# Strided attention and a two-layer MLP on one core: six attention outputs to a bank, first v casts on GpSimd, and the seven-product form one block earlier

## The chip, the core and the metric

The kernel runs on one core of a Trainium2 chip. The core has five engines that work side by side, each with its own queue of instructions taken in order: TensorE (PE in the profile; its weight loads are PEld), VectorE (DVE), ScalarE (ACT), GpSimd (POOL) and SyncE (SP). POOL and SP issue DMAs; POOL's DMAs here load and convert float32 to float16, SP's store the output and transpose tiles on the way. Engines wait for each other through semaphores. The metric is the device time of one execution in microseconds (us).

## What is computed

Eight batches of eight heads, 576 positions of 64 values. Heads 0 to 3 attend to the last 32 positions ("local"), heads 4 to 7 to every earlier position with the same remainder mod 32 ("strided"). The result, with the heads laid side by side, is the input of an MLP:

```
scores = scale * np.matmul(q, k.transpose(0, 1, 3, 2))
...
scores = np.where(masks[None, :, :, :], scores, -1000000000.0)
scores = scores - np.max(scores, axis=-1, keepdims=True)
attn = np.exp(scores)
attn = attn / (np.sum(attn, axis=-1, keepdims=True) + 1e-09)
return np.matmul(attn, v).astype(np.float32)
...
h = x @ w_in
r = np.maximum(h, 0.0)
g = s * (r * r) + b
return (g @ w_out).astype(np.float32)
```

Here x is 4608 x 512, w_in 512 x 2048, w_out 2048 x 512.

## The kernel before

**Attention.** A batch b is worked in four pairs of heads, m = 0 and 1 local, m = 2 and 3 strided; the pair is called (b, m). q and k are brought into transposed form, on PE (`trans`, L427) for the first batches and by DMA transposes from SP for the later ones: `k_dma` (L487, tiles kT_loc, kT_alt, kTs, kT), `q_dma` (L509, tiles qTl, qT). `score` (L551) multiplies them, ACT takes the exponential, and `av` (L614) multiplies by v. v has a column of ones, so the product also holds the sum of the row. A strided pair has 2 heads x 8 tiles of 72 positions. In `av` four tiles of one head go to one PSUM bank (`per = nt // 2`), so a pair is four groups; for each group DVE takes a reciprocal (`rc`) and multiplies (`mu`) into x_nat. A local pair has two groups of six tiles of 96 positions.

**x for the MLP.** x_nat has to be transposed into xT. For local pairs from batch 2 on a DMA does it (`x_dma`, L699). For strided pairs of batches 4 to 6 x_nat is written to DRAM (`x_out`, L691, tile x_dram) and read back transposed (`x_in`, L695); all others, batch 7's strided pairs among them, are transposed on PE (`xtrans`, L665) with one PSUM bank and a copy.

**MLP.** Tokens come in nine blocks T of 512. `ff1` (L904) is 64 matmuls of 512 columns a block; ACT applies the relu, ACT or DVE the square, giving gT. The second product has two forms. `ff2` (L962) is 64 matmuls of 512 columns, with one eviction for each of four row tiles. `ff2_seven` (L784), used from block SEVEN = 3 on, is a Strassen-like form: gT and w_out are cut in quarters, and seven products P1 to P7 of 16 matmuls of 256 columns replace eight. It needs sums of quarters of gT (`sums_post`, L738, eight DVE adds a block, tile S and places in gT), mixed weights (`mix_post`, L768, four DVE subtractions made once; w_mix1 overwrites a quarter of w_out), and eight DVE evictions and adds a block.

**Loads.** POOL's queue is written in order: q, k and v of batch 0, the casts of v_loc (`cast_v`, L362), w_in, then (function `second`) q, k, v of batch 1 and w_out. Later, per batch: a one-element copy `gate` (L1042) that waits until the previous batch's strided k has been transposed by DMA, then ql, kl, qs, ks (`load_qk`), v_loc and v_str. v of the strided heads of batches 0 to 3 lands in a tile vs and is copied to v_str (`cast_v`); for batch 0 ACT or DVE makes that copy.

**Order.** What stands after what on each engine is decided while the kernel is built: `Plan` keeps a clock for PE and a time at which each engine is free, takes steps when their inputs should be ready, and gives a piece of work to the engine that would end it first. It holds estimated costs (`posts`) and arrival times (`AT`, `landing`). Attention steps are paced against MLP steps by `due` (L1223). Where nothing is ready in the first 16 MLP steps, `keep_running` (L1199) puts in dummy matmuls on constants. A change of an estimate can thus reorder all five queues, and SP's queue is in order: a store or a transpose that is not ready holds up all behind it.

Of the kernel before, what the change touches and what calls it, by code (L numbers as in the profile page):

```python
# [10 lines left out]
FP32 = mybir.dt.float32  # L11
# [4 lines left out]
class Plan:  # L16
# [107 lines left out]
def kernel(  # L124
# [237 lines left out]
    def cast_v(b, loc, mm, key):  # L362
        nt, np_, dst = (LT, 128, v_loc) if loc else (ST, SQ, v_str)

        def g(eng):
            src = vl_stage if loc else loaded[b, "vs"].rearrange(
                "p (h t d) -> p h t d", h=4, d=D)
            for h in range(2 * mm, 2 * mm + 2):
                copy_on(eng, out=dst[b % NV][0:np_, h, :, 0:D], in_=src[:, h])
        n = nt * D  # L370
        plan.post([key], {"P": 1000.0} if loc else {"A": 2 * (170 + 0.83 * n), "V": 540.0,
                                                           **({"P": 1500.0} if b == 0 else {})}, g,
                  [("cast", b, mm) if loc else ("in", "vs", b, mm)])
        if loc:
            rows_before(b, mm, ("cast", b, mm))
# [37 lines left out]
    def bank(group):  # L413
        return ps[group.name]

    def pair_steps(b, m):
# [10 lines left out]
        def trans(name, j, group):  # L427
            alone = loc and b < HEAD_T

            def f():  # L430
                if j == 0:
                    st["p" + name] = bank(group).bitcast(FP16)[:, 0:S]
                if alone:
                    for e in range(2):
# [12 lines left out]
            s = Step(f, 70 if alone else 35, needs=[("in", name + sfx, b, mm)],  # L447
                     group=group if j == 0 else None)
            if j == nt - 1:
                key = ("t", name, id_)  # L450
                s.keys = [key]
                if name == "q":
# [3 lines left out]
                    def g(eng):  # L456
                        ps, qD = st["pq"], st["q"]
                        for e in range(2):
# [5 lines left out]
                            else:  # L464
                                copy_on(eng, out=qD[hs, :, e, :],
                                        in_=ps[hs].rearrange("d (j p) -> d j p", j=nt))
                    s.posts = [([key], {"A": 1280, "V": 1520 if loc else 918}, g,
                                [("q", id_), group])]
                else:
                    def g(eng):  # L470
# [5 lines left out]
                        else:  # L476
                            st["k"] = qkp.tile([128, ST, SR], FP16, tag="kTs", name="kTs")
                            copy_on(eng, out=st["k"][:, :, 0:SQ],
                                    in_=st["pk"].rearrange("d (j p) -> d j p", j=nt))
                    s.posts = [([key], {"A": 640, "V": 757 if loc else 453}, g, [("k", id_), group])]  # L480
            return s

        k_by_dma = b >= (KB_DMA if loc else 3)
        q_by_dma = b >= (QB_DMA if loc else QS_DMA)
        x_by_dma = b >= 2 if loc else XS_DMA <= b < B - 1

        def k_dma(eng):  # L487
            if loc:
# [62 lines left out]
        def score(i, group):  # L551
# [18 lines left out]
            if i % per_s == n - 1:  # L570
# [21 lines left out]
                free = [("a", (b - 1, m), 1, nt - 1)] if b else []  # L592
# [18 lines left out]
        per = nt if loc else nt // 2  # L611
        vt = (v_loc if loc else v_str)[b % NV]

        def av(e, j, group):  # L614
            def f():
                if j == 0 and e == 0:
                    st["x"] = xnp.tile([nq, nt, 128], FP16, tag="x" + sfx, name="x_nat")
                if j % per == 0:
                    st["a"] = bank(group)[:, 0:6 * (D + 1)].rearrange("p (j d) -> p j d", d=D + 1)
                g, i = p_of(e, j)  # L620
                nc.tensor.matmul(  # L621
                    out=st["a"][:, j % per, :], lhsT=st["pw", g][0:nk, i * nq:i * nq + WIDE],
                    rhs=vt[0:nk, 2 * mm + e, j, :])
                st["pa", e, j] = st["a"]

            s = Step(f, 35, needs=[("p", id_, p_of(e, j)[0]), ("in", "v" + sfx, b, mm)],
                     group=group if j % per == 0 else None)
            if j % per == per - 1:
                key = ("a", id_, e, j)
                s.keys = [key]  # L630
                j0 = j - per + 1

                def rc(eng):
                    st["rec", e, j] = recp.tile([128, 6, 1], FP32, tag="rec", bufs=8,
                                                name="rec")
                    nc.vector.reciprocal(out=st["rec", e, j][0:nq, 0:per],  # L636
                                         in_=st["pa", e, j][0:nq, 0:per, D:D + 1])

                def mu(eng):
                    if eng == "A":  # L640
                        for i in range(per):
                            nc.scalar.activation(
                                out=st["x"][:, j0 + i, 64 * e:64 * e + 64],
                                in_=st["pa", e, j][0:nq, i, 0:D], func=AF.Copy,
                                scale=st["rec", e, j][0:nq, i])
                        return
                    nc.vector.tensor_tensor(  # L647
                        out=st["x"][:, j0:j0 + per, 64 * e:64 * e + 64],
                        in0=st["pa", e, j][0:nq, 0:per, 0:D],
                        in1=st["rec", e, j][0:nq, 0:per].to_broadcast([nq, per, D]), op=ALU.mult)  # L650

                s.posts = [([key], {"V": 185}, rc, [("r", id_, e, j)]),
                           ([("r", id_, e, j)], {"V": 150 + 1.05 * 64 * per,
                                                 **({"A": 225.0 * per} if b == 0 else {})}, mu,
                            [("x", id_, e, j), group])]
            return s

        for e in range(2):
            for j in range(nt):
                if j % per == 0:  # L660
                    gr = group_of("a", b, m)
                steps.append(av(e, j, gr))
        st["last_av"] = steps[-1]

        def xtrans(j, group):  # L665
            def f():
                if j == 0:
# [5 lines left out]
            jx = j // per * per + per - 1  # L673
            s = Step(f, 35, needs=[("x", id_, 0, jx), ("x", id_, 1, jx)],
                     group=group if j == 0 else None)
            if j == nt - 1:
                key = ("xt", id_)
# [24 lines left out]
                in_=st["x"].rearrange("p t d -> p (t d)"))  # L702

        if x_by_dma and loc:
            plan.post([("x", id_, e, nt - 1) for e in range(2)] + x_free(b), {"D": 1000.0}, x_dma,
                      [("xT", b, m)], 4000.0 if b == B - 1 else 6000.0 if b < 4 else None)
        elif x_by_dma:

            plan.post([("x", id_, e, j) for e in range(2) for j in (per - 1, nt - 1)],
                      {"X": 500.0}, x_out, [("xd", id_)])  # L710
            plan.post([("xd", id_)] + x_free(b), {"Y": 1300.0}, x_in, [("xT", b, m)])
        else:
            gr = group_of("t", b, m)
            for j in range(nt):
# [4 lines left out]
    gts = {}  # L719

    SQ_ACT = 0
    SEVEN = 3
    H = NFT // 2

    def ff_order(T):
# [42 lines left out]
    def mix_post():  # L768

        wl, wr = [[w_out_sb[:, H * j:H * j + H, 256 * k:256 * k + 256] for j in range(2)]  # L770
                  for k in range(2)]
        jobs = ((3, wr[1], wr[0]), (1, wr[0], wl[0]), (2, wr[1], w_mix[1]), (4, wl[1], w_mix[2]))
        before = [("F2", SEVEN - 1)]
        for i, x, y in jobs:
            plan.post(before, {"V": 1250.0},
                      lambda eng, i=i, x=x, y=y: nc.vector.tensor_tensor(
                          out=w_mix[i], in0=x, in1=y, op=ALU.subtract), [("w_mix", i)])
# [301 lines left out]
    def after_landing(i, src):  # L1079
# [7 lines left out]
    early_v(0)  # L1087
    plan.free["P"] = 7100.0
    plan.free["V"] = 6500.0
    AT = {"ql0": 5300.0, "kl0": 6800.0, "ql1": 7750.0, "kl1": 8750.0, "qs": 10150.0,  # L1090
          "ks": 12000.0, "vl0": 7100.0, "vl1": 13300.0, "vs": 14950.0}
    for key, at in AT.items():
        if key[:2] == "vl":
# [209 lines left out]
```

## Time and profile before

| What | us |
|---|---|
| median of 6 runs (lowest to highest) | 306.64 (305.94 to 307.32) |
| the profiled execution | 306.61 |
| its span, first to last instruction | 304.8 |
| last matmul ends, by the timeline | 300.95 |
| last store eviction on DVE ends | 301.47 |

The span is the profiler's; 1.8 us of the execution lie around it. TensorE's granted clock was 1.00 of full speed. Busy time by stage, us of each stretch:

| stretch | PE | DVE | ACT | POOL |
|---|---|---|---|---|
| 0 to 25 | 21.38 | 15.72 | 16.73 | 16.66 |
| 25 to 30 | 2.92 | 1.68 | 2.52 | 2.27 |
| 30 to 50 | 19.96 | 17.17 | 12.76 | 10.49 |
| 50 to 100 | 50.00 | 39.80 | 39.40 | 23.32 |
| 100 to 175 | 75.00 | 57.99 | 53.43 | 35.80 |
| 175 to 200 | 24.29 | 18.35 | 16.65 | 3.87 |
| 200 to 290 | 90.00 | 58.87 | 44.87 | 0 |

A matmul's record reaches from its issue to its modelled end, so records overlap and their mean length is more than the spacing at which they follow each other. For what a matmul costs in a dense stream, the spacing of starts is the number to read.

### The profile page before, as it was taken

Reading aid. Unit: us, or ns where it says so; the run is one execution under the profiler, and the core shown is the slowest. Engines: PE = TensorE matmul, PEld = TensorE weight load, DVE = VectorE, ACT = ScalarE, POOL = GpSimd, SP = SyncE. Lnnn points to the kernel's source line nnn. Section 1 sums busy time; section 2 is a strip of 40 time slices with the busy share of each in tenths; the row PEclk is TensorE's granted clock in tenths of the full one; section 3 lists DMA queues with packets and bytes.
Section 4 is the critical chain, followed back from the end, with each engine's and each line's share of the span. In section 5 each row is a group of like instructions: output and inputs, shape, how many; then the busy total and the mean of one; then the engine's idle time right before and its main releaser. Section 6 shows DMA issues by size and latency. Waiting matters only on the chain.

```text
span 304.8 us, 6780 instructions
## 1 busy us (share of the span) xinstructions
PE 294.5 (97%) x2673; PEld 205.0 (67%) x2673; DVE 216.1 (71%) x482; ACT 186.4 (61%) x331; POOL 92.4 (30%) x135
## 2 busy tenths in 40 slices
PE   7987999999999999999999999999999999999994
PEld 3763655666565667777567776678888676766884
DVE  5655896899777687548886986698766366747653
ACT  4876955889857785658497857685635454444300
POOL 8933463833940392039403940000000000000000
PEclk9999999999999999999999999999999999999999
DMA  8999999998999599999999999946010110300213
GB/s 138 160 207 201 170 209 185 208 150 140 144 151 141 69 126 144 147 171 138 133 197 165 116 141 140 186 103 128 2 37 34 69 37 0 105 0 2 97 62 120
DMA packets 101290, 37.15 MB, mean 122 GB/s; under 512 B 80858, under 2 KB 98778, under 8 KB 101258
## 3 DMA queue, kind: packets, MB, share of 16 engines
q0 software_dynamic: 58880, 18.23, 61.9%
q1 hardware_dynamic: 42378, 18.49, 33.0%
q8 instruction: 21, 0.34, 0.5%
q14 instruction: 11, 0.09, 0.1%
HBM read 36.86 MB, written 10.32 MB: 155 GB/s over the span
## 4 chain that ended last, share of the span: by engine, by line
PE 82%; DMA 12%; POOL 4%; issue 1%; DVE 0%; POOLq 0%
PE ps_f L914 35%; PE ps_f L882 18%; PE ps_f L971 13%; DMA ql<-in_q_dram 5%; PE ps_s L564 5%; DMA v_loc<-in_v_dram 4%; DMA kT_alt<-kl 3%; PE ps_a L621 3%; PE ps_s L882 2%; PE ps_t L882 1%; PE ps_s L971 1%; PE ps_t L444 1%; PE ps_t L621 1%; POOL w_in_sb L335 1%; PE ps_t L669 1%; POOL v_loc L345 1%
## 5 line engine op out<-in xcount | busy, mean ns | idle before, releaser
L914 PE MATMUL ps_f<-xT,w_in_sb 128*128 128x512 f16 (+4 forms) x696 | 148.4, 340 | 0.0
L940 ACT ACTIVATE u<-ps_f 128x512 f16<-128x512 f32 x138 | 81.4, 596 | 70.1 <-PE ps_f L914 67.1
L914 PEld LDWEIGHTS <-w_in_sb 128*128 128x128 f16 x704 | 71.8, 113 | 32.3 <-issue 0.2
L882 PEld LDWEIGHTS <-gT 128*128 128x128 f16 x512 | 48.9, 98 | 11.9
L971 PE MATMUL ps_f<-w_out_sb,gT 128*128 128x512 f16 x176 | 47.8, 379 | 0.0
L950 DVE TENSOR_TENSOR gT<-u 128x1024 f16<-128x1024 f16 x46 | 31.4, 682 | 18.6 <-ACT u L940 18.1
L882 PE MATMUL ps_f<-w_out_sb,gT 128*128 128x256 f16 x312 | 43.4, 272 | 0.0
L948 ACT ACTIVATE gT<-u 128x1024 f16<-128x1024 f16 x26 | 27.5, 1057 | 0.7
L647 DVE TENSOR_TENSOR x_nat<-ps_a,rec 72x256 f16<-72x256 f32 (+1 forms) x55 | 25.2, 459 | 0.9
L971 PEld LDWEIGHTS <-gT 128*128 128x128 f16 x192 | 17.2, 98 | 11.7 <-issue 0.4
L582 ACT ACTIVATE p_str<-ps_s 72x432 f16<-72x432 f32 (+1 forms) x47 | 21.5, 483 | 4.5 <-PE ps_s L564 4.4
L582 ACT ACTIVATE p_loc<-ps_s 128x384 f16<-128x384 f32 x46 | 21.1, 492 | 4.9 <-PE ps_s L564 4.6
L621 PEld LDWEIGHTS <-p_str 72*128 72x128 f16 x256 | 15.2, 98 | 7.5 <-ACT p_str L582 0.7
L754 DVE TENSOR_TENSOR gT<-gT 128x1024 f16<-128x1024 f16 x28 | 18.5, 682 | 1.4 <-ACT gT L948 1.3
L323 POOL DMA_DIRECT2D v_loc<-in_v_dram x24 | 17.7, 760 | 4.3 <-PE ps_a L621 1.8
L882 PE MATMUL ps_f<-w_mix,gT 128*128 128x256 f16 x144 | 18.8, 273 | 0.0
L882 PEld LDWEIGHTS <-S 128*128 128x128 f16 x160 | 15.5, 98 | 3.5
L636 DVE RECIPROCAL rec<-ps_a 72x4 f32<-72x4 f32 (+1 forms) x56 | 10.0, 179 | 9.7 <-PE ps_a L621 9.0
L328 POOL DMA_DIRECT2D v_str<-in_v_dram x16 | 13.0, 816 | 9.3 <-PE ps_f L914 5.4
L1042 POOL COPY gate<-kT 1x1 f16<-1x1 f16 x6 | 1.5, 253 | 44.6 <-DMA kT<-ks 44.6
L345 ACT COPY qD_loc<-ps_t 64x576 f16<-64x576 f16 x18 | 11.4, 632 | 5.6 <-PE ps_t L436 4.7
L882 PE MATMUL ps_f<-w_mix,S 128*128 128x256 f16 x96 | 14.4, 273 | 0.0
(163 smaller groups left out, 415.9 us busy)
## 6 DMA issues: line engine op xcount, KB each, us to landing
out_dram<-o SPq DMA_DIRECT2D x34, 256.0 KB, 2.5
w_in_sb<-in_moe_w_in_dram POOLq DMA_DIRECT2D x4, 512.0 KB, 11.0
w_out_sb<-in_moe_w_out_dram POOLq DMA_DIRECT2D x4, 512.0 KB, 11.5
qs<-in_q_dram POOLq DMA_DIRECT2D x6, 288.0 KB, 6.5
ks<-in_k_dram POOLq DMA_DIRECT2D x6, 288.0 KB, 8.1
v_loc<-in_v_dram POOLq DMA_DIRECT2D x24, 72.0 KB, 8.8
ql<-in_q_dram POOLq DMA_DIRECT2D x5, 288.0 KB, 8.0
kl<-in_k_dram POOLq DMA_DIRECT2D x16, 72.0 KB, 3.6
```

The source lines that it names most:

```text
L323: nc.gpsimd.dma_start(out=vl[LPAD:128, h, :, 0:D], in_=v_band(b, h))
L564: nc.tensor.matmul(out=st["s", g][0:nk, c:c + 2 * nq], lhsT=(st["k"][:, i * nq:i * nq + nk] if loc else st["k"][:, i, 0:SQ]), rhs=st["q"][ ...
L582: nc.scalar.activation(out=st["pw", g][0:nk, 0:2 * n * nq], in_=st["s", g][0:nk, 0:2 * n * nq], func=AF.Exp, scale=scale)
L621: nc.tensor.matmul(out=st["a"][:, j % per, :], lhsT=st["pw", g][0:nk, i * nq:i * nq + WIDE], rhs=vt[0:nk, 2 * mm + e, j, :])
L647: nc.vector.tensor_tensor(out=st["x"][:, j0:j0 + per, 64 * e:64 * e + 64], in0=st["pa", e, j][0:nq, 0:per, 0:D], in1=st["rec", e, j][0:nq, ...
L754: nc.vector.tensor_tensor(out=at(out), in0=at(x), in1=at(y), op=op)
L882: nc.tensor.matmul(out=gts[name, T, t][:, 0] if halves else gts[name, T][:, t], lhsT=lhs(k, t), rhs=rhs(k), start=fresh and k == 0 and (ha ...
L914: nc.tensor.matmul(out=gts["h", T, ft][:, lo:hi], lhsT=w_in_sb[ft // 4][:, ct].rearrange("p (x l) -> p l x", l=4)[:, ft % 4], rhs=xT[ct][: ...
L940: nc.scalar.activation(out=u, in_=gts["h", T, ft], func=AF.Relu)
L948: nc.scalar.activation(out=g, in_=u, func=AF.Square)
L950: nc.vector.tensor_tensor(out=g, in0=u, in1=u, op=ALU.mult)
L971: nc.tensor.matmul(out=gts[id_], lhsT=gts[T][:, ft, ts * 128:(ts + 1) * 128], rhs=w_out_sb[:, ft, cols], start=(ft == 0), stop=(ft == NFT ...
```

## The change

Six edits:

1. In `cast_v` the copies of batch 0's strided v (vs to v_str, four of 72x512) are offered to POOL alone. In the built order they stand on POOL's queue after the four w_in loads and the v_loc copy, and before the loads of batch 1.
2. The copies of q of pair (0, 1) and of k of pair (0, 0) are given to DVE alone.
3. `keep_running` puts in dummies of at least 128 columns into each gap before 9.6 us of the plan's clock. The early estimates (`AT`, the cost of a transpose) are retouched. There are 30 dummy matmuls in the built order instead of 19.
4. Strided outputs: the 16 tiles of a pair go to banks as 6, 6 and 4, in the order n, with the two heads alternating, so a pair has three groups instead of four. x_nat is written across both heads.
5. `XS_DMA <= b` without `< B - 1`: batch 7's strided pairs also go through x_dram, with two stores and two transposing loads on SP in place of 16 transposes on PE.
6. SEVEN = 2: block 2 takes the seven-product form. `mix_post` makes w_mix3, w_mix2 and w_mix4 after block 0's second product and w_mix1 after block 1's.

```diff
-                w = r + self.LATER.get(k[0] if isinstance(k, tuple) else None, 0.0)
+                w = r + self.LATER.get(k[0] if isinstance(k, tuple) and k[2:3] != (0,) else None, 0.0)
...
-        plan.post([key], {"P": 1000.0} if loc else {"A": 2 * (170 + 0.83 * n), "V": 540.0,
-                                                           **({"P": 1500.0} if b == 0 else {})}, g,
+        plan.post([key], {"P": 1000.0} if loc else {"P": 1160.0} if b == 0 else {"A": 2 * (170 + 0.83 * n), "V": 540.0}, g,
...
-                    s.posts = [([key], {"A": 1280, "V": 1520 if loc else 918}, g,
+                    s.posts = [([key], {"V": 1520} if id_ == (0, 1) else {"A": 1280, "V": 1520 if loc else 918}, g,
...
-                    s.posts = [([key], {"A": 640, "V": 757 if loc else 453}, g, [("k", id_), group])]
+                    s.posts = [([key], {"V": 757} if id_ == (0, 0) else {"A": 640, "V": 757 if loc else 453},
+                                g, [("k", id_), group])]
...
-        x_by_dma = b >= 2 if loc else XS_DMA <= b < B - 1
+        x_by_dma = b >= 2 if loc else XS_DMA <= b
...
-        def av(e, j, group):
+        groups = range(2 if loc else 3)
+
+        def av(n, group):
+
+            e, j = divmod(n, nt) if loc else (n % 2, n // 2)
+            g, cnt = n // 6, min(6, 2 * nt - n // 6 * 6)
...
-    SEVEN = 3
+    SEVEN = 2
...
-        jobs = ((3, wr[1], wr[0]), (1, wr[0], wl[0]), (2, wr[1], w_mix[1]), (4, wl[1], w_mix[2]))
-        before = [("F2", SEVEN - 1)]
+        early = [("bcs",)] + ([("F2", SEVEN - 2)] if SEVEN > 1 else [])
+        jobs = ((3, wr[1], wr[0], ALU.subtract, early), (2, w_mix[3], wl[0], ALU.add, []),
+                (4, wl[1], w_mix[2], ALU.subtract, []),
+                (1, wr[0], wl[0], ALU.subtract, [("F2", SEVEN - 1)]))
...
-    AT = {"ql0": 5300.0, "kl0": 6800.0, "ql1": 7750.0, "kl1": 8750.0, "qs": 10150.0,
-          "ks": 12000.0, "vl0": 7100.0, "vl1": 13300.0, "vs": 14950.0}
+    AT = {"ql0": 5200.0, "kl0": 6900.0, "ql1": 7850.0, "kl1": 8700.0, "qs": 10200.0,
+          "ks": 12100.0, "vl0": 7100.0, "vl1": 13450.0, "vs": 15000.0}
...
         n = min(int((until - 100.0 - plan.t) * ghz) - 20, 512) // 128
+        if plan.t < 9600:
+            n = min(max(int((until - plan.t) * ghz / 128 + 0.5), 1), 4)
```

Counts of the built orders, before and after:

| instructions | before | after |
|---|---|---|
| PE, second product, 512 columns | 192 | 128 |
| PE, second product, 256 columns | 672 | 784 |
| PE, transposes of strided x | 80 | 64 |
| PE, dummies | 19 | 30 |
| DVE, reciprocals and DVE multiplies of strided outputs, each group | 4 a pair | 3 a pair |
| DVE, adds for S and gT quarters | 48 | 56 |
| SP, stores and transposing loads through x_dram | 12 | 16 |
| SP, stores of the output | 38 | 38 |

SP's order changes in places too. The stretch in which batch 5's k is transposed reads, in both orders, first before, then after:

```
... xT(4,1), store, kT_alt x2, x_dram (4,2), qT x2, kT x2, x_dram (4,3) ...
... xT(4,1), x_dram (4,2), kT_alt x2, qT x2, kT x2, x_dram (4,3) ...
```

and for batch 7:

```
... qTl x2, store x2, kT_alt x2, x_dram (6,2), qT x2, x_dram (6,3), kT x2 ...
... qTl x2, x_dram (6,2), kT_alt x2, x_dram (6,3), qT x2, kT x2 ...
```

More of the change, by code (lines that the diff above doesn't have):

```diff
@@ L446, in f @@
                     rhs=ident[0:nq, 0:nq], is_transpose=True)
-            s = Step(f, 70 if alone else 35, needs=[("in", name + sfx, b, mm)],
+            s = Step(f, (57 if id_ == (0, 0) else 40) if alone else 35, needs=[("in", name + sfx, b, mm)],
                      group=group if j == 0 else None)
@@ L590, in ms @@
                     nc.vector.tensor_tensor(out=pt[0:nk], in0=pt[0:nk], in1=mask, op=ALU.mult)
-                free = [("a", (b - 1, m), 1, nt - 1)] if b else []
+                free = [("a", (b - 1, m), 1 if loc else 2)] if b else []
                 s.posts = [([key] + free, {"A": 170 + 0.83 * 2 * n * nq}, ex,
@@ L609, in p_of @@
             return i // per_s, i % per_s * 2 + r
-        per = nt if loc else nt // 2
         vt = (v_loc if loc else v_str)[b % NV]
-        def av(e, j, group):
+        groups = range(2 if loc else 3)
+        def av(n, group):
+            e, j = divmod(n, nt) if loc else (n % 2, n // 2)
+            g, cnt = n // 6, min(6, 2 * nt - n // 6 * 6)
             def f():
-                if j == 0 and e == 0:
+                if n == 0:
                     st["x"] = xnp.tile([nq, nt, 128], FP16, tag="x" + sfx, name="x_nat")
-                if j % per == 0:
-                    st["a"] = bank(group)[:, 0:6 * (D + 1)].rearrange("p (j d) -> p j d", d=D + 1)
-                g, i = p_of(e, j)
+                if n % 6 == 0:
+                    st["pa", g] = bank(group)[:, 0:6 * (D + 1)].rearrange("p (j d) -> p j d", d=D + 1)
+                gp_, i = p_of(e, j)
@@ L621, in f @@
                 nc.tensor.matmul(
-                    out=st["a"][:, j % per, :], lhsT=st["pw", g][0:nk, i * nq:i * nq + WIDE],
+                    out=st["pa", g][:, n % 6, :], lhsT=st["pw", gp_][0:nk, i * nq:i * nq + WIDE],
                     rhs=vt[0:nk, 2 * mm + e, j, :])
-                st["pa", e, j] = st["a"]
             s = Step(f, 35, needs=[("p", id_, p_of(e, j)[0]), ("in", "v" + sfx, b, mm)],
-                     group=group if j % per == 0 else None)
-            if j % per == per - 1:
-                key = ("a", id_, e, j)
+                     group=group if n % 6 == 0 else None)
@@ L630, in av, with x_at @@
+            if n % 6 == cnt - 1:
+                key = ("a", id_, g)
                 s.keys = [key]
-                j0 = j - per + 1
+                def x_at(i, k):
+                    if loc:
+                        return st["x"][:, i:i + k, 64 * e:64 * e + 64]
+                    return st["x"].rearrange("p t (e d) -> p (t e) d", e=2)[:, 6 * g + i:6 * g + i + k]
                 def rc(eng):
[L634 to L637, printed above, removed]
+                    st["rec", g] = recp.tile([128, 6, 1], FP32, tag="rec", bufs=8, name="rec")
+                    nc.vector.reciprocal(out=st["rec", g][0:nq, 0:cnt],
+                                         in_=st["pa", g][0:nq, 0:cnt, D:D + 1])
@@ L639, in mu @@
                 def mu(eng):
                     if eng == "A":
-                        for i in range(per):
+                        for i in range(cnt):
                             nc.scalar.activation(
-                                out=st["x"][:, j0 + i, 64 * e:64 * e + 64],
-                                in_=st["pa", e, j][0:nq, i, 0:D], func=AF.Copy,
-                                scale=st["rec", e, j][0:nq, i])
+                                out=x_at(i, 1)[:, 0], in_=st["pa", g][0:nq, i, 0:D], func=AF.Copy,
+                                scale=st["rec", g][0:nq, i])
@@ L646, in mu @@
                         return
                     nc.vector.tensor_tensor(
[L648 to L655, printed above, removed]
@@ L656, in av @@
-            return s
[L658 to L662, printed above, removed]
+                        out=x_at(0, cnt), in0=st["pa", g][0:nq, 0:cnt, 0:D],
+                        in1=st["rec", g][0:nq, 0:cnt].to_broadcast([nq, cnt, D]), op=ALU.mult)
+                s.posts = [([key], {"V": 185}, rc, [("r", id_, g)]),
+                           ([("r", id_, g)], {"V": 150 + 1.05 * 64 * cnt,
+                                              **({"A": 225.0 * cnt} if b == 0 else {})}, mu,
+                            [("x", id_, g), group])]
@@ L663, in pair_steps @@
+            return s
+        for n in range(2 * nt):
+            if n % 6 == 0:
+                gr = group_of("a", b, m)
+            steps.append(av(n, gr))
         st["last_av"] = steps[-1]
@@ L671, in f @@
                     rhs=ident[0:nq, 0:nq], is_transpose=True)
-            jx = j // per * per + per - 1
-            s = Step(f, 35, needs=[("x", id_, 0, jx), ("x", id_, 1, jx)],
+            s = Step(f, 35, needs=[("x", id_, g) for g in (groups if loc else (j // 3,))],
                      group=group if j == 0 else None)
@@ L704, in pair_steps @@
         if x_by_dma and loc:
-            plan.post([("x", id_, e, nt - 1) for e in range(2)] + x_free(b), {"D": 1000.0}, x_dma,
+            plan.post([("x", id_, g) for g in groups] + x_free(b), {"D": 1000.0}, x_dma,
                       [("xT", b, m)], 4000.0 if b == B - 1 else 6000.0 if b < 4 else None)
         elif x_by_dma:
-            plan.post([("x", id_, e, j) for e in range(2) for j in (per - 1, nt - 1)],
-                      {"X": 500.0}, x_out, [("xd", id_)])
-            plan.post([("xd", id_)] + x_free(b), {"Y": 1300.0}, x_in, [("xT", b, m)])
+            plan.post([("x", id_, g) for g in groups],
+                      {"X": 500.0}, x_out, [("xd", id_)],
+                      4000.0 if b == B - 1 else None)
+            plan.post([("xd", id_)] + x_free(b), {"Y": 1300.0}, x_in, [("xT", b, m)],
+                      5000.0 if b == B - 1 else None)
         else:
@@ L771, in mix_post @@
                   for k in range(2)]
-        jobs = ((3, wr[1], wr[0]), (1, wr[0], wl[0]), (2, wr[1], w_mix[1]), (4, wl[1], w_mix[2]))
-        before = [("F2", SEVEN - 1)]
[L774 to L777, printed above, removed]
+        early = [("bcs",)] + ([("F2", SEVEN - 2)] if SEVEN > 1 else [])
+        jobs = ((3, wr[1], wr[0], ALU.subtract, early), (2, w_mix[3], wl[0], ALU.add, []),
+                (4, wl[1], w_mix[2], ALU.subtract, []),
+                (1, wr[0], wl[0], ALU.subtract, [("F2", SEVEN - 1)]))
+        before = []
+        for i, x, y, sign, more in jobs:
+            plan.post(before + more, {"V": 1250.0},
+                      lambda eng, i=i, x=x, y=y, sign=sign: nc.vector.tensor_tensor(
+                          out=w_mix[i], in0=x, in1=y, op=sign), [("w_mix", i)])
             before = [("w_mix", i)]
@@ L1089 @@
     plan.free["V"] = 6500.0
[L1090 to L1091 removed]
+    AT = {"ql0": 5200.0, "kl0": 6900.0, "ql1": 7850.0, "kl1": 8700.0, "qs": 10200.0,
+          "ks": 12100.0, "vl0": 7100.0, "vl1": 13450.0, "vs": 15000.0}
     for key, at in AT.items():
[L1093 removed]
+        if key[0] == "v":
             continue
```

## The prediction, made before the changed kernel was run

> **What bounds it now.** First the page's busy shares, then every wait of PE after the start, then the stream of PE itself.
>
> ```profile
> PE 294.5 (97%) x2673; PEld 205.0 (67%) x2673; DVE 216.1 (71%) x482; ACT 186.4 (61%) x331; POOL 92.4 (30%) x135
> ```
>
> PE is busy 97% of the span; no other engine is near. The waits of PE from 28 us to the end are two, both for DMAs:
>
> ```profile
> PE ps_t L436 <- DMA ql<-in_q_dram: 2.1, 1, 2.1
> PE ps_s L564 <- DMA kT_alt<-kl: 0.7, 1, 0.7
> ```
>
> All else is matmuls back to back. So a change is worth what it takes from PE's queue after 28.76 us, plus what it does to these two waits. The first, in PE's timeline (start, length, then the idle before it in brackets):
>
> ```profile
> 22.85 3.83 PE L914 MATMUL ps_f<-xT,w_in_sb 128*128 128x512 f16 x17
> 28.76 0.45 PE L436 MATMUL ps_t<-ident,ql 96*64 96x96 f16 x12 [2.08 <-DMA ql<-in_q_dram]
> ```
>
> PE is done at 26.68 and waits for batch 1's q. POOL's timeline shows when that load was issued:
>
> ```profile
> 10.34 3.03 POOL L335 DMA_DIRECT2D w_in_sb<-in_moe_w_in_dram  x4
> 13.42 0.72 POOL L345 COPY v_loc<-v_loc 32x640 f16<-32x640 f16 x1
> 14.08 0.68 POOL L298 DMA_DIRECT2D ql<-in_q_dram  x1
> ```
>
> Issued at 14.08, it lands 14.6 us later at 28.7: it stands behind w_in, whose last part (issued at 12.6, landing after up to 14.2) arrives at 26.8. Hence all that makes the start before 26.68 quicker is lost in this wait.
>
> **Price of a matmul.** The chain of waits gives the spacing in a dense stream (start, length of the run):
>
> ```profile
> 142.11 0.86 PE ps_f L971 x4
> 232.82 4.04 PE ps_f L882 x37
> ```
>
> 0.216 us for 512 columns, 0.1092 for 256. In PE's timeline four transposes of 72 columns let the next matmul start 0.13 later: 0.0325 each. Adding such spacings along the built order of PE, from the q transposes at 28.76 on, gives a place in time for every matmul without waits; for the kernel before it ends within 0.8 us of the trace, the 0.7 wait added. Places in the new order below are these sums.
>
> **Seven products for block 2 (edit 6).** Out: 64 x 0.216 = 13.82. In: 112 x 0.1092 = 12.23. On the path, since PE has no slack: **-1.59**. Beside it DVE gets eight adds of 0.68 (L754) and eight evictions and adds of about 0.73 in place of four of 0.75 (L982): 5.4 + 2.8 = 8.3 us more. In the built order these fall between 110 and 150, where DVE is busy 29 of 40 us; the thinner outputs (below) give back about 2 there. The same form runs beside attention from 150 to 175 with DVE busy 21.4 of 25 and no wait of PE, so I take 0; up to 1.5 if DVE comes late for P6. The mixed weights are four DVE operations of 1.2 us either way; three move to 80 to 95, where DVE is busy 10.5 of 15. At 149 to 155 they filled DVE (4.98 of 5) and PE didn't wait: 0.
>
> **Batch 7's strided x by DMA (edit 5).** Out: 16 transposes x 0.0325 = **-0.52** on PE, and two copies off ACT and DVE. In: two stores and two transposing loads on SP, behind nothing but ready stores. The last strided av of batch 7 stands at 213.7 in PE's order, block 7, which needs the result, at 232.8. Multiply 1, store 0.5, landing some 4, load issue 1.3 each and landing 4 to 10 (the other transposes' range) end by 232 at the worst, by 225 as the rows without contention have it; the load queues are empty then (POOL is idle after 182). 0; at most 1.
>
> **Strided outputs 6, 6, 4 (edit 4).** The same 16 matmuls a pair. DVE: before 4 x (0.18 + 0.42) = 2.4, after 2 x (0.18 + 0.55) + 0.6 = 2.06, taking the 96x384 multiply for 72x384: 0.3 a pair less, hidden because DVE isn't the bound. 0.
>
> **The start (edits 1 to 3).** Eleven more dummies, 1920 columns, 0.8 us at 512 columns in 0.216; the DVE/ACT swaps; all before 26.68, covered by 2.08 us of waiting. But the built order now places 34 instead of 32 first-layer matmuls ahead of batch 1's q transposes. The two use w_in's third part, which lands by 24.9 (where POOL's wait for it ends). They run inside the wait: 2 x 0.216 = **-0.43**, if PE gets there by 28.3, so the start may be 1.6 us slower before this is lost.
>
> The v casts on POOL are the part that a rule speaks against. Row: POOL's COPY of 32x640 takes 0.716, so 512 elements 0.573, and four 2.3 us; DVE does one in 0.29, ACT in 0.62. The Trainium skill (GPSIMD Engine Reference, section 3.1) has the vector engine faster for ordinary element work and the best GpSimd loop at 769 ns for 512 elements: four take 3.1. Batch 1's q, k, v loads stand behind them, so ql is issued at 16.4 by the row, 17.2 by the rule; a price of 2.3 or 3.1 if its landing follows its issue. I take 0: w_in is still being moved until 26.8, ten us after either. The ks loads behind already wait for w_in's parts (POOL idle until 18.37, 20.95). v_str is ready by 16.9, where its first matmul stood at 15.87 with a wait of 0.58 later on at 18.41: inside the covered stretch.
>
> **The second wait.** Batch 7's kT_alt. In SP's timeline:
>
> ```profile
> 117.59 0.33 SPq L986 DMA_DIRECT2D out_dram<-o  x1
> 118.03 4.22 SPq L496 DMA_TRANSPOSE kT_alt<-kl  x2
> 122.34 0.50 SPq L692 DMA_DIRECT2D x_dram<-x_nat  x1
> 122.95 4.17 SPq L523 DMA_TRANSPOSE qT<-qs  x2
> 127.22 3.19 SPq L506 DMA_TRANSPOSE kT<-ks  x2
> ...
> 185.16 3.84 SPq L496 DMA_TRANSPOSE kT_alt<-kl  x2
> ```
>
> The kT landing opens POOL's gate (133.63), POOL issues the next batch's loads, these the next transposes: a loop of 30 us a batch. The new order puts x_dram (4,2) ahead of kT_alt of batch 5. Adding the spacings along the new PE order, the last av of (4,2) stands at 121.4; reciprocal, multiply and store bring kT_alt to 123.1, 5.1 later. Behind it queue qT, kT and so POOL's loads for batch 6: the gate slips by 4.4 if all issues stay as long, by 3.2 if those after 131, when the v loads are in, take 1.25 (the shortest seen). In the next round SP reaches batch 6's transposes only at 147 because of stores, and most of the slip is taken up; what comes through is the later v traffic. For batch 7 I take a slip of 2.9, bounds 0 and 4.4.
>
> How it reaches kT_alt: in the trace the first lands at 195.5, 10.1 after issue, just after the last v_str load (issued 181.13, landing after up to 13.8: 194.9), while kT, issued at 194.25, needs 3.2. The skill (DMA: Bandwidth & Descriptors, section SWDGE vs HWDGE vs iDMA) has software and hardware descriptors in different queues that an engine serves in turn. By that rule the transposes share with the loads and needn't slip, the wait goes, -0.71; by the row they follow the loads. I go by the row. Against the slip, PE's new order places that matmul 2.9 us later (168.6 of work after the q transposes instead of 165.7). Wait = 0.71 + slip - 2.9, not below 0: 0.71 again at 2.9, 0 at 0, 2.2 at 4.4. For batch 5 itself kT_alt moves 5.1 later; it landed 5.9 before use and its use is 2.1 later: 2.9 left.
>
> Sum: -1.59 - 0.52 - 0.43 + 0 = **-2.5**. From the profiled execution's 306.61 (median 306.64, so the same): **304.1**.
>
> **Rivals.**
> - *The loop keeps up.* Slip under 2.2: wait gone, 306.6 - 3.2 = 303.4. For: stores leave SP slack before 147. Against: v loads are moved later for certain if the gate slips.
> - *The loop falls behind (slower).* SP's x_dram ahead of kT_alt, and in batch 6 the two x_dram ahead of kT, slip 4.4 and 3.0 and nothing is taken up: 7.4, wait 5.2, 306.6 - 2.5 + 4.5 = 308.6. It decides from a slip of 6.1 on (0.6 us slower). For: the loop had only just become the limit at 195. Against: SP waits for stores, not loads, at 147.
> - *q follows its issue.* POOL's casts bring ql to 31.0: -2.5 + 2.3, 306.4, no change. For: one in-order queue. Against: w_in in front.
> - *DVE late for block 2*: +1.5, 305.6. For: 8 us more on it. Against: 150 to 175.
> - *The seven-product form doesn't save*: its spacing would have to be 0.123; rows say 0.109, so left out.
>
> **Numbers.** 304.1 has 0.55 (own range 303.2 to 305.2), 303.4 0.13, 305.6 0.12, 306.4 0.10, 308.6 0.10. This kernel's measurement tells 0.2%, 0.6 us, from no change. Faster: 0.55 + 0.13 + most of 0.12: 0.78; same 0.12, slower 0.10. For 8 in 10 the range leaves out the slower case and a tail of the best: 302.9 to 306.5.
>
> **What would show it.** PE's wait at ql near 1.6 or less, ending at 28.7 (if at 31, the casts); block 2's L882-type rows at 0.109 spacing without DVE waits; a wait at batch 7's kT_alt of 0 to 2.2, with the gate for batch 6 at 137 to 138; no wait of PE near 230; last matmul near 298.4. Wrong if a new wait stands at batch 5 or 6's scores.

## The result, and the profile after

| | before | after |
|---|---|---|
| median, us (runs) | 306.04 (68) | 305.08 (33) |
| the profiled execution, us | 306.61 | 304.88 |
| its span, us | 304.8 | 303.1 |
| q transposes of batch 1 start at | 28.76 | 28.72 |
| last matmul ends at | 300.95 | 299.12 |

After to before is **0.9961, 95% interval 0.995 to 0.9972**: 1.2 us faster (the medians differ by 0.96). Ratios, here and below, rest on executions within 1.5% of their kernel's fastest, while medians take in all. Between the two profiled executions the difference is 1.7. The forecast was 304.1, or 2.5 less than before, so about half of it (by the ratio) to two thirds (between the profiles) came.

The busy shares of the changed kernel, from its page:

```profile
PE 294.7 (97%) x2716; PEld 210.8 (70%) x2716; DVE 219.5 (72%) x460; ACT 186.5 (62%) x332; POOL 95.7 (32%) x139
```

PE is as busy as before, 97%, in a span 1.7 us shorter. The shares tell no more, so the next view is PE's waits from 28 us to the end (us in total, how often, the longest):

```profile
PE ps_f L625 <- DVE p_loc L590: 1.1, 1, 1.1
PE ps_f L443 <- DVE kp L345: 0.6, 1, 0.6
```

Both waits of before are gone, the 2.1 for q and the 0.7 for kT_alt, and **two new ones for VectorE** stand in their place. In PE's timeline (start, length, idle before it in brackets):

```profile
28.72 0.45 PE L435 MATMUL ps_t<-ident,ql 96*64 96x96 f16 x12
...
42.76 0.37 PE L625 MATMUL ps_f<-v_loc,p_loc 128*128 128x65 f16 x6 [1.15 <-DVE p_loc L590]
...
55.16 0.43 PE L443 MATMUL ps_f<-ident,kp 96*128 96x96 f16 x6 [0.63 <-DVE kp L345]
...
199.34 0.49 PE L564 MATMUL ps_s<-qD_loc,kT_alt 128*128 128x192 f16 x4
```

1.15 and 0.63 make 1.78 us, at a place where the prediction put nothing. The q transposes and the scores on kT_alt have no bracket: PE came to both when the data was there.

From the q transposes to the end of the last matmul PE took 272.19 us before and 270.40 after, 1.79 less. To compare such sums, the stops have to come out, and a stop costs PE more than its bracket says. The bracket counts from the end of the record before it, and that record is longer than the spacing: 0.38 against 0.216 for 512 columns, so about 0.17 a stop (an estimate from these two figures). With every gap and 0.17 for each taken out, the sum is 271.1 before and 268.0 after. The estimate holds well: four traces with the same PE order (the changed kernel and, below, pad_half, pad_ahead and casts_twice), whose gaps add up to between 0.1 and 1.9 us, come to 268.0 within 0.04. A fifth, pad_double, had a granted clock of 0.91 from 30 to 50 us and comes to 269.7.

So PE's own work fell by 3.1 us where 2.54 was forecast; the other 0.6 is not assigned. The two new stops cost 1.78 and twice 0.17, that is 2.1.

**Where the new waits come from.** The chain of waits of the changed kernel names the work (start, length):

```profile
38.92 2.38 DVE v_str L345 x3
...
53.78 1.33 DVE kp L345
```

These are copies by VectorE. Its timeline and POOL's side by side, for the first of them:

```profile
38.71 2.59 DVE L345 COPY v_str<-vs 72x512 f16<-72x512 f16 x4
...
41.99 0.71 DVE L590 TENSOR_TENSOR p_loc<-p_loc,masks 128x1152 f16<-128x1152 f16 x1
```

```profile
38.91 1.83 POOL L307 MEMSET ks<- 16x2048 f16 x1
```

and the same four copies in the kernel before:

```profile
37.94 0.90 DVE L345 COPY v_str<-vs 72x512 f16<-72x512 f16 x4 [0.94 <-DMA vs<-in_v_dram]
39.50 0.74 DVE L590 TENSOR_TENSOR p_loc<-p_loc,masks 128x1152 f16<-128x1152 f16 x1
```

```profile
39.13 1.80 POOL L307 MEMSET ks<- 16x2048 f16 x1
```

Four copies took 0.90 us before and 2.59 after. They now overlap a memset of POOL that clears the 16 padding rows of ks. The view by tile (ns: shortest, median, longest) shows that only one of the four is long:

```profile
L345 DVE COPY v_str<-vs x4: 275/290/1982, 38.7 to 41.0; 72x512 f16<-72x512 f16 x4
```

It is the second, issued at 38.92, just after the memset's start. In the kernel before the memset ran from 39.13, and the copies were done at 38.84: 0.3 us apart. The change put VectorE at the copies 0.77 later and POOL at the memset 0.22 earlier. The mask multiply at 41.99, which PE waits for, stands behind the copies in VectorE's queue. The second wait is of the same kind:

```profile
53.70 1.40 DVE L345 COPY kp<-kl 96x768 f16<-96x768 f16 x1
```

```profile
53.09 1.80 POOL L307 MEMSET qs<- 16x2048 f16 x1
```

A copy of this shape takes 0.35 where no memset runs (at 52.40 in pad_ahead, below). This one ends at 55.10, 0.21 after the memset's end at 54.89.

The Trainium skill (SBUF — State Buffer, section "Who interferes with whom") states what such a pair would do: a VectorE copy can go into a mode that uses the port pair which VectorE shares with GpSimd; the pair is an exclusive lock, held by whichever started first for its whole instruction. One copy that lasts until just past the memset's end, between others of 0.28, is what that would look like. The page also states that a VectorE instruction with two inputs in SBUF is in the way only of a GpSimd operation that reads SBUF, and a memset reads nothing. That agrees with the trace of before: under its memset (39.13 to 40.93) the mask multiply at 39.50 took 0.74, as elsewhere. The prediction didn't use this page. The traces show when a copy is long, not the port itself.

### The profile page after: what moved, and what is told of

Its sections match the earlier page's. It is cut to its first block, busy times and chain, and to the rows that moved or that the text cites. A ratio compares the mean times of both kernels' runs of the same rounds, so it can differ in the third digit from the quotient of the medians.

```text
span 303.1 us, 6851 instructions
## 1 busy us (share of the span) xinstructions
PE 294.7 (97%) x2716; PEld 210.8 (70%) x2716; DVE 219.5 (72%) x460; ACT 186.5 (62%) x332; POOL 95.7 (32%) x139
## 4 chain that ended last, share of the span: by engine, by line
PE 90%; DMA 3%; POOL 3%; DVE 3%; issue 1%; DVEq 0%; POOLq 0%
PE ps_f L921 40%; PE ps_f L889 25%; PE ps_f L978 8%; PE ps_s L564 4%; DMA w_in_sb<-in_moe_w_in_dram 3%; PE ps_a L625 2%; PE ps_s L889 2%; PE ps_t L625 1%; PE ps_t L889 1%; PE ps_s L978 1%; PE ps_t L443 1%; DVE v_str L345 1%; PE ps_f L443 1%; PE ps_s L921 1%; PE ps_t L672 1%
## 5 line engine op out<-in xcount | busy, mean ns | idle before, releaser
L889 PEld LDWEIGHTS <-gT 128*128 128x128 f16 x608 | 58.1, 98 | 12.9
L889 PE MATMUL ps_f<-w_out_sb,gT 128*128 128x256 f16 x376 | 53.3, 273 | 0.0
L957 DVE TENSOR_TENSOR gT<-u 128x1024 f16<-128x1024 f16 x42 | 28.7, 684 | 16.0 <-ACT u L947 15.5
L955 ACT ACTIVATE gT<-u 128x1024 f16<-128x1024 f16 x30 | 31.8, 1058 | 0.8
L978 PE MATMUL ps_f<-w_out_sb,gT 128*128 128x512 f16 x112 | 29.4, 379 | 0.1
L652 DVE TENSOR_TENSOR x_nat<-ps_a,rec 96x384 f16<-96x384 f32 (+2 forms) x46 | 23.8, 518 | 0.7
L889 PE MATMUL ps_f<-w_mix,gT 128*128 128x256 f16 x176 | 23.9, 273 | 0.0
L758 DVE TENSOR_TENSOR gT<-gT 128x1024 f16<-128x1024 f16 x34 | 22.4, 681 | 1.4 <-ACT gT L955 1.3
L978 PEld LDWEIGHTS <-gT 128*128 128x128 f16 x128 | 11.5, 98 | 9.8 <-issue 0.7
L642 DVE RECIPROCAL rec<-ps_a 96x6 f32<-96x6 f32 (+2 forms) x46 | 8.4, 182 | 12.7 <-PE ps_a L625 12.5
L625 PEld LDWEIGHTS <-p_str 72*128 72x128 f16 x256 | 13.3, 98 | 5.5
```

The lines of the kernel that those rows point to most:

```text
L625: nc.tensor.matmul(out=st["pa", g][:, n % 6, :], lhsT=st["pw", gp_][0:nk, i * nq:i * nq + WIDE], rhs=vt[0:nk, 2 * mm + e, j, :])
L652: nc.vector.tensor_tensor(out=x_at(0, cnt), in0=st["pa", g][0:nq, 0:cnt, 0:D], in1=st["rec", g][0:nq, 0:cnt].to_broadcast([nq, cnt, D]), o ...
L758: nc.vector.tensor_tensor(out=at(out), in0=at(x), in1=at(y), op=op)
L889: nc.tensor.matmul(out=gts[name, T, t][:, 0] if halves else gts[name, T][:, t], lhsT=lhs(k, t), rhs=rhs(k), start=fresh and k == 0 and (ha ...
L955: nc.scalar.activation(out=g, in_=u, func=AF.Square)
L957: nc.vector.tensor_tensor(out=g, in0=u, in1=u, op=ALU.mult)
```

## The experiments

Eight variants follow, each of which computes the whole result. Ratios are to the kernel before on the same chip.

### The memsets made half as long

```diff
-                nc.gpsimd.memset(ts[64:SR], 0.0)
+                nc.gpsimd.memset(ts[64:SR].bitcast(FP32), 0.0)
```

Same bytes, half as many elements, so POOL should hold them for half the time.

> The changed kernel with GpSimd's zeroing of the pad rows of ks and qs (16x2048 f16, 1.80 to 1.83 us, four times) written as 16x1024 float32, so half as many elements; order of all other queues unchanged. Theory A (GpSimd's memset locks VectorE's copies out): memsets of about 0.95; the v_str copy at 38.9 ends with the memset near 39.9 instead of 40.9, PE's wait before v_loc/p_loc of batch 1 falls from 1.15 to about 0.2, the wait at kp (0.63) goes; span 303.1 - 1.5 = 301.6 and a ratio to the kernel before of about 0.991. Theory B (VectorE merely has too much queued there, the long copy is chance): the long copy and both waits stay, ratio 0.996.

Measured: 303.83 us, ratio 0.9933 [0.9911, 0.9954]. The interval leaves out both 0.991 and 0.996. The trace says why it lies between. The four v_str copies and the kp copy, in VectorE's timeline:

```profile
39.23 0.90 DVE L345 COPY v_str<-vs 72x512 f16<-72x512 f16 x4
...
52.56 1.20 DVE L345 COPY kp<-kl 96x768 f16<-96x768 f16 x1
```

```profile
38.39 0.97 POOL L307 MEMSET ks<- 16x1024 f32 x1
52.60 0.94 POOL L307 MEMSET qs<- 16x1024 f32 x1
```

```profile
PE ps_f L443 <- DVE kp L345: 0.4, 1, 0.4
```

The memset takes 0.95 instead of 1.80. The v_str copies run at 0.90 again and PE's wait of 1.15 is gone. kp is still caught: it was issued with the memset and ended 0.22 after it, and PE waits 0.4 for it. Besides that, the start was 0.5 us later than in the changed kernel's execution (q transposes at 29.19, without a wait for q). From there to the last matmul PE took 268.59, that is 1.81 less than in the changed kernel, though one small wait was left.

### The memsets made twice

```diff
                 nc.gpsimd.memset(ts[64:SR], 0.0)
+                nc.gpsimd.memset(ts[64:SR], 0.0)
```

> The changed kernel with each of the four pad memsets made twice in a row (3.6 us of GpSimd instead of 1.8). Theory A: VectorE's copy that meets it takes up to 3.8 us or two copies take 2 each, PE's wait before v_loc/p_loc of batch 1 grows from 1.15 to about 2.9 and the wait at kp grows by up to 1.8; ratio about 1.005 to 1.008. Theory B: copies of 0.28 as elsewhere or one chance long one, ratio 0.996 to 0.998 (loads 1.8 later have cover).

Measured: median 310.32 us, ten executions spread from 305.11 to 311.78; ratio 1.0045 [1.0004, 1.0086], from the four shortest. A's range began at 1.005, just above this ratio and inside its interval; B's ended at 0.998. The size in time is thus uncertain. The profiled execution took 310.65, so only its waits are read. The two longest of PE from 28 us on, and the copies:

```profile
PE ps_f L626 <- DVE p_loc L591: 3.1, 1, 3.1
PE ps_f L444 <- DVE kp L346: 1.2, 1, 1.2
```

```profile
38.75 4.32 DVE L346 COPY v_str<-vs 72x512 f16<-72x512 f16 x4
```

```profile
L346 DVE COPY v_str<-vs x4: 276/1150/1982, 38.7 to 42.8; 72x512 f16<-72x512 f16 x4
```

Four copies of 0.28 take 4.32 beside 3.7 us of memset, because two of them are now long, 1.98 each: one for each memset. The wait behind them grows from 1.15 to 3.1. PE's waits after a VectorE copy thus follow the memset's length in both directions.

### The memsets moved ahead of the loads

In `load_qk` the tile is taken and its padding cleared, as float32, before the ql and kl loads are issued; PE, ACT, DVE and SP keep the changed kernel's order.

```diff
+        pads = {}
+        for name in ("q", "k"):
+            if name == "k" and b in (2, 3):
+                pads[name] = ks[b % 2]
+            elif name == "q" and b in (QS_DMA, QS_DMA + 1):
+                pads[name] = inp.tile([SR, NS], FP16, tag="qs", name="qs")
+            if name in pads:
+                nc.gpsimd.memset(pads[name][64:SR].bitcast(FP32), 0.0)
...
-            if name == "k" and b in (2, 3) or name == "q" and b in (QS_DMA, QS_DMA + 1):
-                nc.gpsimd.memset(ts[64:SR], 0.0)
```

> The changed kernel with the pad memsets as 16x1024 float32 and moved ahead of the ql and kl loads of the same batch on GpSimd's queue, so that they run while VectorE reads PSUM or multiplies masks. PE, ACT, DVE and SP orders unchanged. Theory A: no copy of VectorE is caught, both waits of PE go (1.7 us), span about 301.4, ratio 0.990 to 0.991; this would beat both kernels. Theory B: 0.996.

Measured: 303.1 us, ratio **0.9903 [0.9872, 0.9935]**, span 301.0: faster than both kernels. POOL's memset is now at 33.44 and the copies are free of it:

```profile
33.44 0.95 POOL L295 MEMSET ks<- 16x1024 f32 x1
```

```profile
38.17 1.03 DVE L353 COPY v_str<-vs 72x512 f16<-72x512 f16 x4
...
52.40 0.35 DVE L353 COPY kp<-kl 96x768 f16<-96x768 f16 x1
```

No wait for a VectorE copy is left after 28 us. (The four v_str copies take 1.03, not 0.90, as one of them takes 0.42; why was not looked into.) What is left is one for the load of w_out, 0.8 at 39.73, which the other kernels show smaller or not at all (PE came to this matmul at 38.93 here, at 39.59 in the changed kernel):

```profile
PE ps_f L986 <- DMA w_out_sb<-in_moe_w_out_dram: 0.8, 1, 0.8
```

### The same in the kernel before

The edit of pad_ahead, made in the kernel before. If a memset costs anything by being there, and not by meeting a copy, it should help here too.

> The kernel before, with its four memsets as 16x1024 float32 and ahead of the ql and kl loads of their batch; PE, ACT, DVE and SP orders as before. Theory A (a memset costs time only where a copy of VectorE meets it, and in the kernel before the v_str copies end at 38.84, just ahead of the memset at 39.13): PE's waits after 28 us stay the two for ql (2.1) and kT_alt (0.7), ratio 0.998 to 1.001. Theory B (the memset costs the kernel before too, by POOL's later loads or by DVE at large): ratio 0.993 to 0.996.

Measured: 306.25 us, ratio 0.9995 [0.9975, 1.0014]. No gain. A holds for the time. Its detail on the waits does not: the 0.7 for kT_alt isn't there, that for q is 0.2 instead of 2.1 as PE came to it later, and one of 0.4 for an exponential is new; from the q transposes to the last matmul it is 272.10, against 272.19. Nor are the copies all free: the edit put a memset on the kp copy at 50.26, which took 1.41, but PE did not wait for it. So the memsets cost the kernel before nothing that can be measured, and the changed kernel some 1.8 us (0.9961 to 0.9903).

### Edit 6 undone

```diff
-    SEVEN = 2
+    SEVEN = 3
```

> The changed kernel with SEVEN = 3 again, all else of the change kept. If edit 6 is worth its count (-1.6 of PE's queue, no waits of its own): about 1.6 us slower than the changed kernel, ratio to before about 1.001. If VectorE's adds for block 2 eat it: ratio 0.996 as the changed kernel. Where the two waits on VectorE near 42 and 55 come from the memsets and not from the form, they stay or move with the order.

Measured: 306.86 us, ratio 1.0006 [0.9977, 1.0036], against 0.9961 for the changed kernel: edit 6 is worth about 1.4 us, though the intervals nearly touch. In the traces PE takes 271.63 from the q transposes to the last matmul here, with 1.6 of waits in it (0.6 at the same mask multiply; v_str copies 2.62 long), and 270.40 with 1.78 in the changed kernel: 270.03 and 268.62 without waits, a difference of 1.41; with 0.17 more for every stop it is 1.5. The count said 1.59. The first memset meets the v_str copies here too, so it was edits 1 to 5 that brought them together; which of these, no run shows. The kp copy, issued 0.4 us ahead of its memset here, took 0.55 and PE did not wait for it.

### The casts on POOL made twice

From here on the base is pad_ahead, so that no memset is in the way. Batch 0's v_str casts are made twice, which sends batch 1's loads off later.

```diff
-                copy_on(eng, out=dst[b % NV][0:np_, h, :, 0:D], in_=src[:, h])
+                for _ in range(2 if b == 0 and not loc else 1):
+                    copy_on(eng, out=dst[b % NV][0:np_, h, :, 0:D], in_=src[:, h])
```

> pad_ahead, with the four casts of batch 0's v_str on POOL made twice: ql is issued 2.3 us later, at 19.8. Theory A (ql lands behind w_in, whenever it is issued): ql's transposes start within 0.7 us of 28.1 and the ratio stays within 0.002 of pad_ahead's 0.990. Theory B (a landing follows its issue): they start at about 30.3, ratio 0.997 to 0.998.

Measured: 303.71 us, ratio 0.991 [0.9887, 0.9932], level with pad_ahead. The trace needs care: the q transposes start at 30.41, which is what B expects. But they have no wait for q. When q landed is read on POOL, which holds back its next-but-some load until ql is in:

```profile
14.59 4.98 POOL L353 COPY v_str<-vs 72x512 f16<-72x512 f16 x8 [0.19 <-DMA vs<-in_v_dram]
19.51 0.69 POOL L306 DMA_DIRECT2D ql<-in_q_dram  x1
...
28.18 0.56 POOL L321 DMA_DIRECT2D vs<-in_v_dram  x1 [0.84 <-DMA ql<-in_q_dram]
```

Issued at 19.51, in by 28.2. By the same row it was in by 28.4 in the changed kernel (issued 16.81), 28.1 in pad_ahead (17.50), 28.3 in casts_free (14.71). Over all ten kernels the issue lies between 14.1 and 19.5 and this row between 27.7 and 29.0, in no order with the issue: the kernel before, with the earliest issue, has the latest row. A holds for q. PE was late for other reasons: a wait of 0.5 for the doubled casts that pad_ahead doesn't have, and a granted clock of 0.70 between 20 and 25 us in this execution.

### Edit 1 undone

```diff
-        plan.post([key], {"P": 1000.0} if loc else {"P": 1160.0} if b == 0 else {"A": 2 * (170 + 0.83 * n), "V": 540.0}, g,
+        plan.post([key], {"P": 1000.0} if loc else {"A": 2 * (170 + 0.83 * n), "V": 540.0, **({"P": 1500.0} if b == 0 else {})}, g,
```

> pad_ahead with edit 1 undone: the v_str casts of batch 0 go to ACT or DVE, and the planner's order changes with it (0.5 us more of PE work ahead of the end by the count). Theory A (the casts on POOL cost nothing, since ql lands behind w_in): q transposes at about 28, ratio 0.990 to 0.994. Theory B (the casts delay ql and with it PE): transposes at 26 to 27, ratio 0.985 to 0.988.

Measured: 305.39 us, ratio 0.996 [0.9944, 0.9977]: neither. B is out, since q was in no earlier (28.3, above), and A's range ended at 0.994. Without edit 1 the kernel is slower by some 1.7 us than pad_ahead. That the casts on POOL are what is good is not shown, since the planner orders all queues anew here. The trace gives the parts. PE is 1.26 later at the q transposes, but this execution was 1.3 behind already at the first matmul on qD_str and kTs, ahead of the first place where PE's order differs:

```profile
16.09 0.25 PE L572 MATMUL ps_f<-qD_str,kTs 128*72 128x144 f16 x1 [0.42 <-DVE kTs L353]
```

In pad_ahead that matmul stands at 14.76. So the late start is this execution's own. From the q transposes on PE took 1.1 longer, of which the order's count explains 0.5.

### Edit 5 undone

```diff
-        x_by_dma = b >= 2 if loc else XS_DMA <= b
+        x_by_dma = b >= 2 if loc else XS_DMA <= b < B - 1
```

> pad_ahead with edit 5 undone: batch 7's strided x goes back to 16 transposes on PE. Theory A (edit 5 is worth its matmuls, 16 x 0.0325): last matmul 0.5 us later, ratio 0.0015 above pad_ahead's, 0.9915 to 0.9925. Theory B (the two transposing loads cost as much elsewhere, or the work is hidden): no change, 0.990.

Measured: 302.93 us, ratio 0.9889 [0.987, 0.9909]. No loss can be seen; the intervals of the two overlap almost whole. PE's own stream does show the matmuls. Its order is the same in both up to a matmul that starts at 211.91 in pad_ahead and at 212.14 here; from that start to the end of the last matmul PE takes 85.64 here and 85.11 in pad_ahead, and 85.11 too in the changed kernel, pad_half, pad_double and casts_twice. That is 0.53 for the 16 transposes, where the count said 0.52. The sums from the q transposes (269.05 here, 268.97 in pad_ahead) hide it, because pad_ahead's wait for w_out, at 39.7 and so far ahead of edit 5's place, is 0.54 longer. The time does not resolve 0.5 us: that edit 5 shortens PE's stream is shown, that it shortens the kernel is not.

## Why the prediction was right, and where it was wrong

- **The bound.** Right: PE's queue after 28.7 us set the end in all kernels.
- **The wait for q.** q came no later (in by 28.4, though issued 2.7 us later than before), and casts_twice shows that its landing doesn't follow its issue. Four casts took 2.27 us; the row gave 2.3, the rule 3.1. w_in's third part came in time, though not for the reason given: the idle time of POOL that ends at 24.90 in the kernel before is put down to VectorE there. But the spare of 1.6 us that the step allowed was used up: PE ran at half rate (512 columns every 0.42 us) until 9.9 us and came to q at 28.72 without a wait. The added dummies, priced at 0.216 for 512 columns, stand mostly in that stretch, where they cost about twice that (nine of 512 columns took 3.59 from 1.05 us on). The -0.43 was just kept. In pad_half, with the same order, PE was 0.5 later still, and that went straight into the time.
- **Edit 6.** -1.59 expected, 1.4 to 1.5 measured. VectorE was busy 33.2 us from 110 to 150, 4.2 more than before (6 were expected), and PE didn't wait for it there.
- **Edit 5.** The loads at the end were hidden, as expected. The -0.52 is seen in PE's stream (0.53), not in the time.
- **Edit 4.** 0 expected; no wait of PE is tied to it. It was not tried by itself.
- **The loop.** The gate for batch 6's loads opened at 133.97 and 135.34, 0.3 and 1.2 us later than before, not 3.2 to 4.4. That for batch 7's loads opened 3.0 and 4.6 us later, more than the 2.9 taken, and kT_alt was issued 2.5 later:

```profile
187.62 0.80 POOL L328 DMA_DIRECT2D v_str<-in_v_dram  x1 [2.67 <-PE ps_f L921]
```

```profile
187.63 3.59 SPq L496 DMA_TRANSPOSE kT_alt<-kl  x2
```

  PE used kT_alt at 199.34 without a wait, while the last v_str load, issued at 187.62, needs at least 14.1 to land: 201.7. So kT_alt does not follow the loads; the step that read this from the row of before was wrong. Why the wait of 0.71 did not stay is less sure. PE came 11.7 us after kT_alt's issue. Without the two new stops (2.1) it would have come some 9.6 after it. In the kernel before kT_alt was in 10.4 after its issue; in before_pads_ahead, issued at 185.50 and used at 194.84 without a wait, within 9.3. So the new stops may have hidden what was left of this wait. pad_ahead, which has no waits for copies, has none for kT_alt either, but there it was issued 2.1 us earlier than in the changed kernel.
- **The step that failed** is the first sum, "So a change is worth what it takes from PE's queue after 28.76 us, plus what it does to these two waits". It has no term for a new wait on VectorE, and the zeros under it ("so I take 0" for block 2, "hidden because DVE isn't the bound" for edit 4, "all before 26.68" for edits 1 to 3) look at how busy VectorE is where work is added or moved. For block 2 the zero held. The cost, 1.78 us by the brackets, came at 39 and 53 us, where nothing was added to VectorE's count, because copies that had stood 0.3 us clear of a memset now met it. The rival *DVE late for block 2* had nearly the right size (+1.5), in the wrong place and for the wrong cause.

The misses offset each other in part: on one side the 0.71 that did not stay and 0.6 of PE's work that fell without having been forecast, on the other 2.1 for the new stops. The forecast was 0.8 below the profiled execution. That the time lies inside the range of 302.9 to 306.5 is in part luck, the more so as the new stops may have hidden the old wait.

## What to carry to other kernels

Before trusting that a reordering costs nothing on VectorE, list GpSimd's longer memsets and copies with their times, and see which VectorE copies stand within a microsecond of them: a busy share can't show it. Clear padding early, ahead of the loads and away from copies, and through a wider type where the bytes allow it; here that was worth some 1.8 us (0.9961 to 0.9903), against 1.4 to 1.5 for edit 6. Judge a wait removed at the start only after measuring how late the start can be in several executions.

## What the hardware showed that was not expected

- **A caught copy ends with the memset.** In six kernels a VectorE copy of q or k was caught by a POOL memset (in before_pads_ahead and casts_free by the second of two in a row), and each ended 0.21 or 0.22 us after it: in the changed kernel 55.10 after 54.89, pad_half 53.76 after 53.54, before_pads_ahead 51.67 after 51.45, casts_twice 51.22 after 51.00, casts_free 51.73 after 51.51, pad_double 54.96 after 54.75. Of the four short v_str copies one memset catches one, which ends 0.16 after it; two memsets catch two. The mask multiply was not caught.
- **A memset that met a copy under way took longer.** In seven_from_3 the kp copy was issued at 52.74, the memset started at 53.12 and took 1.91 instead of 1.80.
- **A memset on POOL went by elements in the one pair measured.** 16x2048 as float16 takes 1.80, the same bytes as 16x1024 float32 0.95.
- **The start's rate differs between executions.** With the same order on PE there, a run of seven dummies (five of 128 columns and two of 512; the line prints the first one's shape) took 1.57 us in the changed kernel and 0.88 in seven_from_3:

```profile
5.82 1.57 PE L1221 MATMUL ps_s<-w_mix 128*128 128x128 f16 x7
```

```profile
5.88 0.88 PE L1221 MATMUL ps_s<-w_mix 128*128 128x128 f16 x7
```

  The granted clock is 1.00 in both profiles there. The Trainium skill (TensorE: Matmul & The Clock Gate, "Part 1: The HAM clock gate") has the first warm-up depend on a window that runs freely, so that the number of slow matmuls differs from run to run. That the number differs agrees. The length does not: the page has some 3.4 us of sustained work end the slow stretch, while in the changed kernel's execution it reached from the first matmul at 1.05 to 9.9 us, with one idle gap of 0.55 that ended at 5.20. What ends it no run here shows.
